# Head steps of a sliding-window attention kernel: a bank for the value product, and score maxima head by head in three banks

## The chip, the cores and the metric

The kernel runs on one core of a Trainium2 chip. The metric is the device time of one execution in microseconds (us). Before the change three runs took 2301.49, 2301.74 and 2302.6 us; the median is 2301.74.

A core has engines that run side by side, each with its own queue of instructions in program order: PE (TensorE) multiplies matrices, and PEld is its loading of weights; DVE (VectorE), ACT (ScalarE) and POOL (GpSimd) work on elements; SP issues the DMA transfers. PE writes into PSUM, which has eight banks of 512 fp32 columns on 128 partitions. Engines wait for each other on semaphores.

## The reference

Four layers act on x of 2048 rows and 640 columns; layers 1 and 3 are attention, layers 2 and 4 Fourier mixing:

```python
qkv = (x @ wqkv).reshape(B, S, 3, H, Dh).transpose(2, 0, 3, 1, 4)   # H = 32, Dh = 20
scores = einsum("bhqd,bhkd->bhqk", q, k) * Dh ** -0.5
mask = (idx[:, None] - idx[None, :] >= 0) & (idx[:, None] - idx[None, :] < 256)
p = softmax(where(mask, scores, -1e9))
o = einsum("bhqk,bhkd->bhqd", p, v).transpose(0, 2, 1, 3).reshape(B, S, D) @ wo
...
x = x + A(layernorm(x)); x = x + F(layernorm(x)); x = x + A(layernorm(x)); x = x + F(layernorm(x))
```

The change touches only the two attention layers. Each query row sees at most 256 keys, which is three blocks of 128 keys.

## The kernel before

**Quads, blocks and steps.** The 32 heads are taken in eight groups of four, called quads here (NQ = 8), and the 2048 rows in 16 blocks of 128 (NB = 16). A step of `heads` handles one block of one quad, so a layer has 128 steps. Of the four heads, two (z = 0 and 1) times two (e = 0 and 1), the index e says on which half of PE's rows a head's q and k lie (rows 0 or 64 onward): matmuls of different e can run side by side.

**Three strands in a step.** Each step serves three places at once. Strand s runs ten steps ahead (LEAD): `s_head` (the matmul at L545) computes the scores of one query block against up to three key blocks, and `s_max` takes the row maximum under the mask. For three key blocks `s_max` works on two heads, that is two banks, at once: L558 overwrites the masked part of the third block with a copy of the first, and L561 takes the maximum over columns 128 to 384. For the first two blocks of a quad (one or two key blocks) it runs one instruction per head, L564, which adds the mask, takes the maximum and leaves it in `mc`, and writes the masked scores to a scratch tile `ux` that nobody reads. Every four steps `m_rows` transposes the maxima of four blocks on PE (L571), copies them negated to `mt` on ACT (L574), and two DMAs (L576) put them as an extra row beside q. Strand t: `t_head` (L585) computes the scores transposed, with keys on the partitions and the maximum subtracted by that extra row; `t_exp` (L594, ACT) takes the exponential into `pt`; `t_mask` (L600, L604, POOL) sets masked entries to zero. Strand v is one step behind t: `pv` (L615) multiplies by the values of four heads side by side, each on 32 columns of PE, and L622 on ACT copies the result into `ou`.

**Banks.** Transposed scores go to banks 0 and 1, scores for maxima to banks 2 and 3 (z = 0) and 4 and 5 (z = 1). Bank 2 also takes the value product in its columns 384 to 512, and the transposition of `m_rows` in its first 128. Projections and other fill work use banks 6 and 7, and others while they are free; the table ROLES lists them.

**The order in a step** is written out by hand at the end of `heads`: for each z the four score matmuls in the order t (e=0), s (e=1), t (e=1), s (e=0), then `s_max`, `t_exp` and `t_mask`; after z = 0 comes `fill`, which issues a portion of other matmuls (the projections of later quads, L189, and later the partial sums of the output projection, whose results are added at L861); after z = 1 come the transposition (every fourth step), `pv` and the copy of the transposition. Work put off with `post` is issued some half steps later by `tick`. In the first head stage a fill has eight matmuls of 512 columns, in every fourth step six; in the late stage, when the projections are done, it has some 18 of 320 columns. `copied` (L474 on DVE, L476 on ACT, then L477 and L478 on POOL) empties a projection's banks every eight steps; L636 on DVE takes the reciprocals of the softmax sums every four steps.

Of the kernel before, what the change touches and what calls it, by code (L numbers as in the profile page):

```python
# [10 lines left out]
U16 = mybir.dt.uint16  # L11
AF = mybir.ActivationFunctionType
OP = mybir.AluOpType
AX = mybir.AxisListType
# [3 lines left out]
P = 128  # L18
# [9 lines left out]
NEG = -1.0e30  # L28
# [14 lines left out]
CHUNKS = ((0, 16, 0, 8), (0, 16, 8, 16), (16, 24, 0, 16), (24, 32, 0, 16), (0, 32, 16, 20))  # L43

ROLES = {
    "m": (6, 7), "f": (6, 7, 0, 1), "w": (3, 4, 5, 7),
    "q": (0, 1), "v": (5, 6, 7), "x4": (2, 3), "x1": (4,),
    "o": (5, 6),
    "y": (5, 6, 7, 0), "x1h": (4, 1),
# [12 lines left out]
class Net:  # L62
# [66 lines left out]
    def next(self, name):  # L129
        i = self.turn.get(name, 0)  # L130
        self.turn[name] = i + 1
        tiles = getattr(self, name)[:3]
        return tiles[i % len(tiles)]
# [387 lines left out]
    def heads(self, xsrc, xdst, hook):  # L521
        nc = self.nc
        qp = [t.rearrange("p (z s) -> p z s", z=2) for t in self.qp]
# [13 lines left out]
                                  self.vd[n // 4][:, n % 4 * 4:n % 4 * 4 + 4, :])  # L537

        mc = {}

        def s_head(quad, qb, z, e):
            n = min(qb + 1, 3)
            k0 = qb - n + 1
            b = 64 * e
            nc.tensor.matmul(  # L545
                self.banks[:, 2 + 2 * z + e, :n * P], qp[quad % 2][b:b + 60, z, qb * P:(qb + 1) * P],
                kp[quad % 2][b:b + 60, z, k0 * P:(qb + 1) * P], start=True, stop=True)

        def s_max(quad, qb, z):


            n = min(qb + 1, 3)
            if qb % 4 == 0 and z == 0:
                mc[quad, qb // 4] = pool.tile([P, 2, 2, 4], F32, name="mc", tag="mc")
            out = mc[quad, qb // 4][:, z, :, qb % 4]
            p = self.banks[:, 2 + 2 * z:4 + 2 * z, :]
            if n == 3:
                nc.vector.copy_predicated(  # L558
                    p[:, :, 256:384], self.mask[:, 256:].bitcast(U16).unsqueeze(1).broadcast_to([P, 2, P]),
                    p[:, :, :128])  # L560
                nc.vector.tensor_reduce(out=out, in_=p[:, :, 128:384], op=OP.max, axis=AX.X)  # L561
                return
            for e in range(2):
                nc.vector.tensor_tensor_reduce(  # L564
                    out=self.ux[:, :n * P], in0=p[:, e, :n * P], in1=self.mask[:, 384 - n * P:], scale=1.0, scalar=NEG,
                    op0=OP.add, op1=OP.max, accum_out=out[:, e:e + 1])

        def m_rows(quad, u):
            m = mc.pop((quad, u))
            p = self.banks[:16, 2, :P]  # L570
            nc.tensor.transpose(p, m.rearrange("p z e j -> p (z e j)"), self.ident)  # L571
            mt = pool.tile([16, P], F32R, name="mt", tag="mt", bufs=1)
            yield
            nc.scalar.activation(mt, p, AF.Copy, scale=-1.0)  # L574
            for z in range(2):
                self.post(1, lambda z=z: nc.sync.dma_start(  # L576
                    qp[quad % 2][60:125:64, z, u * 512:(u + 1) * 512].bitcast(F32),
                    mt[8 * z:8 * z + 8, :].bitcast(F32)))
# [3 lines left out]
        def t_head(quad, kb, z, e):  # L582
            n = min(NB - kb, 3)
            b = 64 * e
            nc.tensor.matmul(  # L585
                self.banks[:, e, :n * P], kp[quad % 2][b:b + 61, z, kb * P:(kb + 1) * P],
                qp[quad % 2][b:b + 61, z, kb * P:(kb + n) * P], start=True, stop=True)
# [19 lines left out]

        def pv(quad, qb):

            p = self.banks[:, 2, 384:]  # L610
            for kb in range(max(qb - 2, 0), qb + 1):
                t = pt[quad, kb]
                vq = self.vq[(4 * quad + kb // 4) % 3]
                for h in range(4):
                    nc.tensor.matmul(  # L615
                        p[32 * h:32 * h + 32, :], vq[:, 96 * (kb % 4) + 21 * h:96 * (kb % 4) + 21 * h + 32],
                        t[:, h, (qb - kb) * P:(qb - kb + 1) * P], start=kb == max(qb - 2, 0), stop=kb == qb,
                        tile_position=(0, 32 * h), skip_group_check=True)
            pt.pop((quad, qb - 2), None)
            if qb % 4 == 0:  # L620
                now_ou[0] = self.next("ou")
            nc.scalar.activation(now_ou[0][:, qb % 4 * P:qb % 4 * P + P], p, AF.Copy)  # L622
            if qb % 4 == 3:
                finish(quad, qb // 4, now_ou[0])

        now_ou = [None]

        def finish(quad, bk, ou):
            sm = pool.tile([P, 16], F32, name="sm", tag="sm")
            rc = pool.tile([P, 16], F32, name="rc", tag="rc")  # L630
            cols = slice(bk * 512, (bk + 1) * 512)
            at = (2, 7, 9) if quad < NQ - 1 else (1, 5, 6)
            self.post(at[0], lambda: nc.sync.dma_start(sm, ou[0:P:32, :]))
            self.post(at[0], lambda: nc.sync.dma_start(
                self.od[4 * quad:4 * quad + 4, :, cols].rearrange("h r s -> (h r) s"), ou))
            self.post(at[1], lambda: nc.vector.reciprocal(out=rc, in_=sm))  # L636

            def store():
                nc.sync.dma_start(
                    self.rd[bk, 4 * quad:4 * quad + 4, :].rearrange("h (a b) -> (h a) b", b=16), rc)  # L640
                self.stored.add((quad, bk))
            self.post(at[2], store)
# [33 lines left out]
        def fill(n):  # L676

            k, size = 0, 1
            while k < size:
                r = more()  # L680
                if r == 0 and k == 0:
                    continue
                if r != 1:
                    return
                k += 1
                if k == 1:
                    left = self.left + 1
                    size = -(-left // max(1, round(left / n)))
            if self.left == 0:
                more()  # L690
                relieve()
# [3 lines left out]
        steps = 16 * NQ  # L695
        for step in range(-LEAD, steps + 1):
            now[0] = step
            self.wide, self.lead, self.tiled = step + LEAD > steps, step < -2, step < steps - 1
            for f in later.pop(step, []):
                f()  # L700
            s, t, v = step + LEAD, step, step - 1
            if due and s >= due[0][0]:
                while done[0] < due[0][1]:
                    fill(15)
                due.pop(0)
                q, j = (s + AHEAD) // 16, (s + AHEAD) % 16 // 4
                for i, f in enumerate(self.pack(q, j)):
                    defer(i // 3, f)
                for f in later.pop(step, []):
                    f()  # L710
            if v >= 0 and v % 4 == 3:
                load_v(v // 4 + 2)
            if done[0] < total:
                nf = max([FIRST if t < 0 else RATE]
                         + [(d - done[0]) / max(1, at - s) for at, d in due])
            elif made[0] < early:
                nf = LATE
            else:
                nf = LATE
            rows = ((s - 1) // 16, ((s - 1) % 16) // 4) if 4 <= s < steps + 4 and s % 4 == 0 else None  # L720
            for z in range(2):
                for e in range(2):
                    if 0 <= t < steps:
                        t_head(t // 16, t % 16, z, e)
                    if 0 <= s < steps:
                        s_head(s // 16, s % 16, z, 1 - e)
                if 0 <= s < steps:
                    s_max(s // 16, s % 16, z)
                if 0 <= t < steps:
                    for e in range(2):  # L730
                        t_exp(t // 16, t % 16, z, e, e + 1)
                    t_mask(t // 16, t % 16, z)
                if z:
                    m = m_rows(*rows) if rows else iter(())
                    next(m, None)
                    if 0 <= v < steps:
                        pv(v // 16, v % 16)
                    for _ in m:
                        pass
                if z == 0 and t >= 0 or t < -1 or t >= steps:  # L740
                    fill(nf)
                self.tick()
            if step >= steps:
                self.load_to(step - steps + 2)
            if step > 16 * (NQ - 1):
                self.poll_late(step - 16 * (NQ - 1))
# [794 lines left out]
```

## Time and profile before

| What | us |
|---|---|
| median of three runs | 2301.74 |
| span of the profiled execution, from the first to the last instruction | 2300.9 |
| first head stage of the first attention layer | 172 to 440 |
| late head stage of the first attention layer | 456 to 534 |
| the same stages of the second attention layer | 1318 to 1580 and 1600 to 1675 |

The profile is one execution. A row of a group reads: line, engine, operation, written tile <- read tiles, shapes, count | busy us, mean ns of one | idle time of the engine just before, and what ended most of it. A row of the waits reads: who waited <- for whom: us in total, times, longest. A row of the timeline reads: start us, duration us, engine, line, operation, and in brackets the idle time before it. Starts of matmuls are recorded, their ends are modelled. The tile `banks` is the whole of PSUM, so rows don't name the bank.

### The profile page before, as it was taken

The numbers are of one execution on the slowest core, as the hardware profiler recorded it, in microseconds if no ns is written. First come the engines' busy times: TensorE is split into PE (matmuls) and PEld (weight loads), VectorE is DVE, ScalarE is ACT, GpSimd is POOL, SyncE is SP. The second block draws the span as 40 slices with busy tenths as digits, with TensorE's granted clock in tenths as the row PEclk, the third lists the DMA queues.
The fourth block names the chain that finished last, engine by engine and source line by source line (L and its number), as shares of the span: only waits on it lengthen the run. The fifth ranks groups of instructions, "written<-read, shape, count | busy, mean of one in ns | idle before, by whom it ended". The sixth has DMA issues, their size and how long they took to land.

```text
span 2300.9 us, 48611 instructions
## 1 busy us (share of the span) xinstructions
PE 2209.8 (96%) x18064; PEld 1844.4 (80%) x18064; DVE 1499.6 (65%) x2841; ACT 1114.3 (48%) x2497; POOL 1019.9 (44%) x1540
## 2 busy tenths in 40 slices
PE   8999999999889999999999999999988899999999
PEld 7977777677758888889999777776777688888899
DVE  6357777675688768772451677776747978688622
ACT  2117666666454545541331266666665545445310
POOL 3036666767745223230130466667677442331300
PEclk9999999999999999999999999999999999999999
DMA  5545556774535354655455455657744344546452
GB/s 189 173 148 168 182 166 192 218 195 146 175 112 176 126 179 137 212 166 177 149 168 181 144 183 166 190 185 218 199 153 151 111 164 142 178 141 214 157 171 98
DMA packets 217293, 385.53 MB, mean 168 GB/s; under 512 B 38880, under 2 KB 85472, under 8 KB 217056
## 3 DMA queue, kind: packets, MB, share of 16 engines
q1 hardware_dynamic: 217056, 382.43, 51.8%
q8 instruction: 142, 2.33, 0.4%
q14 instruction: 95, 0.78, 0.1%
HBM read 267.39 MB, written 113.77 MB: 166 GB/s over the span
## 4 chain that ended last, share of the span: by engine, by line
PE 39%; POOL 4%; DVE 3%; DMA 2%; ACT 2%; issue 1%; SPq 0%; POOLq 0%; ACTq 0%
PE banks L1234 14%; PE banks L171 11%; PE banks L189 5%; PE banks L615 3%; PE banks L585 3%; PE banks L545 2%; POOL big L164 1%; DMA qk_d<-c 1%; POOL c L478 0%; POOL x L783 0%; POOL pt L604 0%; DVE mc L561 0%; POOL kp L164 0%; POOL ou L1163 0%; POOL pt L600 0%
## 5 line engine op out<-in xcount | busy, mean ns | idle before, releaser
L594 ACT ACTIVATE pt<-banks 128x384 f32<-128x384 f32 (+2 forms) x1024 | 425.9, 468 | 191.4 <-PE banks L585 151.6
L545 PE MATMUL banks<-kp,qp 60*128 60x384 f32 (+2 forms) x1024 | 370.3, 381 | 3.8 <-DVE mc L561 1.9
L561 DVE TENSOR_REDUCE mc<-banks 128x2 f32<-128x512 f32 x448 | 310.4, 693 | 15.4
L600 POOL TENSOR_SCALAR_AFFINE_SELECT pt<-pt 128x256 f32<-128x256 f32 x512 | 208.8, 408 | 246.2 <-ACT pt L594 195.9
L189 PE MATMUL banks<-big,wc 64*128 64x512 f32 x1920 | 306.1, 402 | 0.4 <-DVE pt L372 0.4
L558 DVE COPY_PREDICATED banks<-mask,banks 128x256 f32<-128x256 uint16 x448 | 191.6, 428 | 152.8 <-PE banks L545 138.8
L585 PE MATMUL banks<-qp,kp 61*128 61x384 f32 (+2 forms) x1024 | 257.6, 363 | 7.9 <-ACT pt L594 7.0
L615 PE MATMUL banks<-pt,vq 128*32 128x128 f32 x5760 | 216.9, 279 | 17.2 <-DVE mc L561 11.9
L545 PEld LDWEIGHTS banks<-kp,qp 60*128 60x128 f32 x1024 | 182.6, 186 | 47.6 <-ACT ou L622 22.5
L189 PEld LDWEIGHTS banks<-big,wc 64*128 64x128 f32 x1920 | 210.5, 187 | 10.8 <-DVE pt L372 0.5
L615 PEld LDWEIGHTS banks<-pt,vq 128*32 128x32 f32 x5760 | 145.0, 110 | 78.6 <-DVE mc L561 46.1
L585 PEld LDWEIGHTS banks<-qp,kp 61*128 61x128 f32 x1024 | 148.9, 187 | 71.2 <-ACT pt L594 40.2
L164 DVE TENSOR_TENSOR qp<-pt,qp 128x512 fp32r<-128x512 f32 (+1 forms) x209 | 168.9, 816 | 47.8 <-ACT qp L158 46.9
L604 POOL TENSOR_SCALAR_AFFINE_SELECT pt<-pt 128x256 f32<-128x256 f32 x448 | 182.9, 408 | 0.0
L158 ACT ACTIVATE qp<-pt 128x512 fp32r<-128x512 f32 (+1 forms) x209 | 128.9, 624 | 99.5 <-DVE pt L1164 33.0
L1234 PE MATMUL banks<-qp,big 128*128 128x512 f32 x630 | 152.9, 393 | 6.1 <-POOL big L164 4.2
L1163 POOL TENSOR_TENSOR pt<-pt,pt 128x512 f32<-128x512 f32 x40 | 60.5, 1516 | 206.5 <-DMA pt<-c 148.0
L1422 DVE TENSOR_TENSOR x<-banks,x 128x320 f32<-128x320 f32 x64 | 29.7, 488 | 178.5 <-DMA x<-x_d 117.1
L1234 PEld LDWEIGHTS banks<-qp,big 128*128 128x128 f32 x630 | 118.2, 189 | 31.8 <-POOL big L164 5.7
L158 ACT ACTIVATE c<-pt 128x512 fp32r<-128x512 f32 x144 | 88.3, 624 | 75.0 <-DVE pt L1160 36.6
L164 DVE TENSOR_TENSOR c<-pt,c 128x512 fp32r<-128x512 f32 x140 | 110.1, 798 | 14.9 <-ACT c L158 12.6
L171 PE MATMUL banks<-big,pt 128*128 128x320 f32 x768 | 118.2, 309 | 0.7 <-DVE pt L1359 0.7
(204 smaller groups left out, 4527.7 us busy)
## 6 DMA issues: line engine op xcount, KB each, us to landing
pt<-c SPq DMA_DIRECT2D x188, 512.0 KB
qk_d<-c SPq DMA_DIRECT2D x80, 512.0 KB
kp<-qk_d SPq DMA_DIRECT2D x384, 80.0 KB
qp<-qk_d SPq DMA_DIRECT2D x384, 80.0 KB
kp<-u_d SPq DMA_DIRECT2D x32, 640.0 KB
o_d<-ou SPq DMA_DIRECT2D x64, 256.0 KB
x_d<-x SPq DMA_DIRECT2D x48, 320.0 KB
v_d<-pt SPq DMA_DIRECT2D x16, 768.0 KB
```

Source lines behind the costliest of these rows:

```text
L158: nc.scalar.activation(hi, src, AF.Copy, scale=-1.0 if neg else 1.0)
L164: (eng or nc.vector).tensor_tensor(out=lo, in0=src, in1=hi.bitcast(F32), op=OP.subtract)
L171: self.nc.tensor.matmul(p, x, y, start=n == 0, stop=n == last)
L189: self.nc.tensor.matmul(ps[a], x[r], y[r], start=half + i == 0, stop=half == 1 and i == n - 1, skip_group_check=True)
L545: nc.tensor.matmul(self.banks[:, 2 + 2 * z + e, :n * P], qp[quad % 2][b:b + 60, z, qb * P:(qb + 1) * P], kp[quad % 2][b:b + 60, z, k0 * P: ...
L558: nc.vector.copy_predicated(p[:, :, 256:384], self.mask[:, 256:].bitcast(U16).unsqueeze(1).broadcast_to([P, 2, P]), p[:, :, :128])
L561: nc.vector.tensor_reduce(out=out, in_=p[:, :, 128:384], op=OP.max, axis=AX.X)
L585: nc.tensor.matmul(self.banks[:, e, :n * P], kp[quad % 2][b:b + 61, z, kb * P:(kb + 1) * P], qp[quad % 2][b:b + 61, z, kb * P:(kb + n) * P ...
L594: nc.scalar.activation(pt[quad, kb][:, 2 * z + e0:2 * z + e1, :n * P], self.banks[:, e0:e1, :n * P], AF.Exp, scale=SCALE)
L600: nc.gpsimd.affine_select(out=t[:, :, 0:P], in_=t[:, :, 0:P], pattern=[[0, 2], [1, P]], compare_op=OP.is_ge, fill=0.0, base=0, channel_mul ...
L615: nc.tensor.matmul(p[32 * h:32 * h + 32, :], vq[:, 96 * (kb % 4) + 21 * h:96 * (kb % 4) + 21 * h + 32], t[:, h, (qb - kb) * P:(qb - kb + 1 ...
L1234: nc.tensor.matmul(self.banks[:, bk, :], p, b[q], start=start and m == 0, stop=stop and last and m == 2, skip_group_check=True)
```

## The change

The value product gets bank 5, each block of four at its own 128 columns, and ACT copies two blocks at a time, after every second one. The scores for maxima go to banks 2, 3 and 4 in turn, one bank a head (`s_bank`), and mask and maximum are one instruction per head for every block; it follows its score matmul directly in `s_head`, and `s_max` is gone. The transposition of the maxima takes a turn among the same three banks, and is issued, whole, after the value product. In the second half of each z the order of the two matmuls is exchanged: t (e=0), s (e=1), s (e=0), t (e=1). In the role "w", used once the score strand has ended, bank 2 replaces bank 5.

```diff
--- before.py
+++ after.py
@@ -43,7 +43,7 @@
 CHUNKS = ((0, 16, 0, 8), (0, 16, 8, 16), (16, 24, 0, 16), (24, 32, 0, 16), (0, 32, 16, 20))
 
 ROLES = {
-    "m": (6, 7), "f": (6, 7, 0, 1), "w": (3, 4, 5, 7),
+    "m": (6, 7), "f": (6, 7, 0, 1), "w": (2, 3, 4, 7),
     "q": (0, 1), "v": (5, 6, 7), "x4": (2, 3), "x1": (4,),
     "o": (5, 6),
     "y": (5, 6, 7, 0), "x1h": (4, 1),
@@ -537,40 +537,32 @@
                                   self.vd[n // 4][:, n % 4 * 4:n % 4 * 4 + 4, :])
 
         mc = {}
+        turn = [0]
+
+        def s_bank():
+            turn[0] += 1
+            return 2 + turn[0] % 3
 
         def s_head(quad, qb, z, e):
+
             n = min(qb + 1, 3)
             k0 = qb - n + 1
             b = 64 * e
+            p = self.banks[:, s_bank(), :n * P]
             nc.tensor.matmul(
-                self.banks[:, 2 + 2 * z + e, :n * P], qp[quad % 2][b:b + 60, z, qb * P:(qb + 1) * P],
+                p, qp[quad % 2][b:b + 60, z, qb * P:(qb + 1) * P],
                 kp[quad % 2][b:b + 60, z, k0 * P:(qb + 1) * P], start=True, stop=True)
-
-        def s_max(quad, qb, z):
-
-
-            n = min(qb + 1, 3)
-            if qb % 4 == 0 and z == 0:
+            if (quad, qb // 4) not in mc:
                 mc[quad, qb // 4] = pool.tile([P, 2, 2, 4], F32, name="mc", tag="mc")
-            out = mc[quad, qb // 4][:, z, :, qb % 4]
-            p = self.banks[:, 2 + 2 * z:4 + 2 * z, :]
-            if n == 3:
-                nc.vector.copy_predicated(
-                    p[:, :, 256:384], self.mask[:, 256:].bitcast(U16).unsqueeze(1).broadcast_to([P, 2, P]),
-                    p[:, :, :128])
-                nc.vector.tensor_reduce(out=out, in_=p[:, :, 128:384], op=OP.max, axis=AX.X)
-                return
-            for e in range(2):
-                nc.vector.tensor_tensor_reduce(
-                    out=self.ux[:, :n * P], in0=p[:, e, :n * P], in1=self.mask[:, 384 - n * P:], scale=1.0, scalar=NEG,
-                    op0=OP.add, op1=OP.max, accum_out=out[:, e:e + 1])
+            nc.vector.tensor_tensor_reduce(
+                out=self.ux[:, :n * P], in0=p, in1=self.mask[:, 384 - n * P:], scale=1.0, scalar=NEG,
+                op0=OP.add, op1=OP.max, accum_out=mc[quad, qb // 4][:, z, e, qb % 4:qb % 4 + 1])
 
         def m_rows(quad, u):
             m = mc.pop((quad, u))
-            p = self.banks[:16, 2, :P]
+            p = self.banks[:16, s_bank(), :P]
             nc.tensor.transpose(p, m.rearrange("p z e j -> p (z e j)"), self.ident)
             mt = pool.tile([16, P], F32R, name="mt", tag="mt", bufs=1)
-            yield
             nc.scalar.activation(mt, p, AF.Copy, scale=-1.0)
             for z in range(2):
                 self.post(1, lambda z=z: nc.sync.dma_start(
@@ -607,7 +599,7 @@
 
         def pv(quad, qb):
 
-            p = self.banks[:, 2, 384:]
+            p = self.banks[:, 5, qb % 4 * P:qb % 4 * P + P]
             for kb in range(max(qb - 2, 0), qb + 1):
                 t = pt[quad, kb]
                 vq = self.vq[(4 * quad + kb // 4) % 3]
@@ -619,7 +611,9 @@
             pt.pop((quad, qb - 2), None)
             if qb % 4 == 0:
                 now_ou[0] = self.next("ou")
-            nc.scalar.activation(now_ou[0][:, qb % 4 * P:qb % 4 * P + P], p, AF.Copy)
+            if qb % 2:
+                cs = slice(qb % 4 * P - P, qb % 4 * P + P)
+                nc.scalar.activation(now_ou[0][:, cs], self.banks[:, 5, cs], AF.Copy)
             if qb % 4 == 3:
                 finish(quad, qb // 4, now_ou[0])
 
@@ -720,23 +714,19 @@
             rows = ((s - 1) // 16, ((s - 1) % 16) // 4) if 4 <= s < steps + 4 and s % 4 == 0 else None
             for z in range(2):
                 for e in range(2):
-                    if 0 <= t < steps:
-                        t_head(t // 16, t % 16, z, e)
-                    if 0 <= s < steps:
-                        s_head(s // 16, s % 16, z, 1 - e)
-                if 0 <= s < steps:
-                    s_max(s // 16, s % 16, z)
+                    heads = [(t_head, t, e), (s_head, s, 1 - e)]
+                    for head, n, i in heads[::-1] if e else heads:
+                        if 0 <= n < steps:
+                            head(n // 16, n % 16, z, i)
                 if 0 <= t < steps:
                     for e in range(2):
                         t_exp(t // 16, t % 16, z, e, e + 1)
                     t_mask(t // 16, t % 16, z)
                 if z:
-                    m = m_rows(*rows) if rows else iter(())
-                    next(m, None)
                     if 0 <= v < steps:
                         pv(v // 16, v % 16)
-                    for _ in m:
-                        pass
+                    if rows:
+                        m_rows(*rows)
                 if z == 0 and t >= 0 or t < -1 or t >= steps:
                     fill(nf)
                 self.tick()
```

## The prediction

> **What bounds the kernel now.** I read the page first, then the table of waits, then the two head stages instruction by instruction, because an average over the span hides which wait closes a step.
>
> ```profile
> span 2300.9 us, 48611 instructions
> PE 2209.8 (96%) x18064; PEld 1844.4 (80%) x18064; DVE 1499.6 (65%) x2841; ACT 1114.3 (48%) x2497; POOL 1019.9 (44%) x1540
> L561 DVE TENSOR_REDUCE mc<-banks 128x2 f32<-128x512 f32 x448 | 310.4, 693 | 15.4
> ...
> L558 DVE COPY_PREDICATED banks<-mask,banks 128x256 f32<-128x256 uint16 x448 | 191.6, 428 | 152.8 <-PE banks L545 138.8
> ```
>
> PE looks full, but its ends are modelled, and a matmul that waits behind another can count as busy. So the waits at the head lines matter more than the 96%:
>
> ```profile
> PEld banks L615 <- DVE mc L561: 46.1, 120, 1.4
> PEld banks L545 <- ACT ou L622: 22.5, 134, 0.2
> PEld banks L545 <- ACT mt L574: 17.2, 55, 0.3
> PEld banks L571 <- DVE mc L561: 10.4, 36, 0.3
> ```
>
> Four waits return in nearly every step, and all four go over bank 2: the value product (L615) and the transposition (L571) wait for the maximum that reads banks 2 and 3, and the next score (L545) waits for the copies that empty bank 2. One ordinary step of the first head stage:
>
> ```profile
> 251.84 0.44 PE L585 MATMUL banks<-qp,kp 61*128 61x384 f32 x1
> 252.13 0.34 PE L585 MATMUL banks<-qp,kp 61*128 61x384 f32 x1
> 252.31 0.44 PE L545 MATMUL banks<-kp,qp 60*128 60x384 f32 x1
> 252.32 1.36 PE L189 MATMUL banks<-big,wc 64*128 64x512 f32 x8
> 252.79 0.43 DVE L558 COPY_PREDICATED banks<-mask,banks 128x256 f32<-128x256 uint16 x1 [0.51 <-PE banks L545]
> 253.25 0.69 DVE L561 TENSOR_REDUCE mc<-banks 128x2 f32<-128x512 f32 x1
> 253.35 0.33 PE L545 MATMUL banks<-kp,qp 60*128 60x384 f32 x1
> 253.52 0.34 PE L585 MATMUL banks<-qp,kp 61*128 61x384 f32 x2
> 253.70 0.33 PE L545 MATMUL banks<-kp,qp 60*128 60x384 f32 x1
> 254.00 0.86 PE L615 MATMUL banks<-pt,vq 128*32 128x128 f32 x24
> 254.79 0.38 PE L585 MATMUL banks<-qp,kp 61*128 61x256 f32 x1
> 254.93 0.28 ACT L622 ACTIVATE ou<-banks 128x128 f32<-128x128 f32 x1
> 255.26 0.44 PE L545 MATMUL banks<-kp,qp 60*128 60x384 f32 x1
> ```
>
> This is a closed loop: score 252.31, mask and maximum 252.79 to 253.94 (253.25+0.69), value product 254.00, its copy 254.93 to 255.21, next score 255.26. In sum 0.48+1.15+0.06+0.93+0.28+0.05 = 2.95 us, exactly the step. Neither PE nor DVE is full in it (DVE idles 0.51); the latency of the loop sets the step.
>
> **The change, part by part.**
>
> *Own bank for the value product; the transposition takes a turn among the score banks.* The loop is cut. What would PE need without it? The last score of the first half could follow the matmul at 252.13 on the other rows instead of coming at 252.31 (0.18). The value product could follow the score of 253.70 after one more interval as between 253.52 and 253.70 (0.18), so at some 253.9 instead of 254.00 (0.09). The step falls to 2.95-0.27 = 2.68. The eight projection matmuls take 253.35-252.32 = 1.03, 0.26 a pair; in four steps one step has six instead of eight (-0.26) and one a transposition (an estimate of 0.2, a little over a score's 0.18, since a weight load and a change of rows go with it). Four steps are some 4x2.68-0.26+0.2 = 10.7 us, sixteen some 42.6. Sixteen steps take today:
>
> ```profile
> 218.46 0.41 PE L615 MATMUL banks<-pt,vq 128*32 128x128 f32 x6
> ...
> 266.18 0.38 PE L615 MATMUL banks<-pt,vq 128*32 128x128 f32 x5
> ```
>
> that is 47.72 us (the product of a group's first block, then of the next group's). On PE alone, sixteen steps would win 5.1 us.
>
> *One mask-and-maximum instruction per head.* It has never run on 384 elements here, but the first two blocks of each group use it on 128 and 256:
>
> ```profile
> 231.95 0.29 DVE L564 CUSTOM_DVE_ANT_0 ux<-banks,mask 128x128 bf16<-128x128 f32 x1 [0.60 <-PE banks L545]
> 232.29 0.29 DVE L564 CUSTOM_DVE_ANT_0 ux<-banks,mask 128x128 bf16<-128x128 f32 x1
> ...
> 235.07 0.42 DVE L564 CUSTOM_DVE_ANT_0 ux<-banks,mask 128x256 bf16<-128x256 f32 x1 [1.25 <-PE banks L545]
> 235.43 0.08 DVE L564 DVE_READ_ACCUMULATOR2_ANT mc<- 128x1 f32 x1
> 235.54 0.42 DVE L564 CUSTOM_DVE_ANT_0 ux<-banks,mask 128x256 bf16<-128x256 f32 x1
> 235.89 0.08 DVE L564 DVE_READ_ACCUMULATOR2_ANT mc<- 128x1 f32 x1
> 236.12 0.42 DVE L564 CUSTOM_DVE_ANT_0 ux<-banks,mask 128x256 bf16<-128x256 f32 x1
> 236.47 0.08 DVE L564 DVE_READ_ACCUMULATOR2_ANT mc<- 128x1 f32 x1
> 236.59 0.42 DVE L564 CUSTOM_DVE_ANT_0 ux<-banks,mask 128x256 bf16<-128x256 f32 x1
> ...
> 235.75 0.28 PE L545 MATMUL banks<-kp,qp 60*128 60x256 f32 x1
> ```
>
> Each head is two DVE instructions, the sweep and the read of its accumulator. From start to start a pair takes 0.34 on 128 and 0.47 on 256 elements; the same 0.13 more gives 0.60 on 384. That is the lower bound. But the interval 235.54 to 236.12 is 0.58, 0.11 longer. The third sweep is the first of its pair: it waits for PE as well as for the sweep before it, whose scratch ux it overwrites. The score at 235.75 ended at 236.03, 0.09 before it, while the predicated copy above follows its score (252.31+0.44 = 252.75) by 0.04; so PE alone doesn't explain the 0.11, and I read most of it as the price of waiting for two engines. After the change every head has both waits. Upper bound: 0.60+0.11 = 0.71 per head. I take 0.71, since the new instruction is of the kind of the one that shows it.
>
> Sixteen steps hold 56 heads of 384, four of 256 and four of 128: 56x0.71+4x0.58+4x0.45 = 43.9 us of DVE. Between them come two projection copies, priced by the predicated copy that follows one:
>
> ```profile
> 247.96 0.68 DVE L474 COPY x<-banks 128x512 f32<-128x512 f32 x1
> 248.56 0.42 DVE L558 COPY_PREDICATED banks<-mask,banks 128x256 f32<-128x256 uint16 x1
> ```
>
> 2x0.60 = 1.2, and four reciprocals, which I estimate at 0.15 each beside the accumulator read, 0.6. DVE needs 45.7 us of sixteen steps, against 42.6 on PE: DVE becomes the bound. For bubbles I add 0.3 (the transposition holds one of three banks for part of a step). 46.0 against 47.72: 1.7 us won per sixteen steps. The lower bound 0.60 gives 56x0.60+4x0.47+4x0.34+1.8 = 38.6, below PE's 42.6.
>
> The Trainium skill, VectorE: DVE Perf Modes, section "The DRAIN you can't avoid", reports that chained Vector instructions with a semaphore after each took as long as with one at the end. By that rule 0.60 would hold; the interval 235.54 to 236.12 here speaks against it, and the rule's result is the first rival.
>
> *Three banks in turn instead of four in pairs.* A head waits for the maximum three heads earlier. With DVE the bound, PE runs ahead until the banks are full; three waiting heads are 2.1 us of DVE work. PE's longest absence is the fill: 0.17 for the score before it, 1.03, and 0.48 from a score to DVE, 1.7. Three banks cover that by 0.4, so I price the rotation at nothing in this stage. In the late stage, where the fill is longer, the cover is thin:
>
> ```profile
> 172.00:440.00 268.00, 262.76 (x3422) 199.47 (x3419) 199.43 (x439) 187.02 (x496) 183.31 (x398) 1.00 0.58 181
> ...
> 456.00:534.00 78.00, 75.03 (x1058) 58.98 (x1057) 58.84 (x126) 48.31 (x128) 52.78 (x99) 1.00 0.70 191
> ...
> L861 DVE TENSOR_TENSOR big<-banks,big 128x320 f32<-128x320 f32 x22 | 9.8, 486 | 0.9 <-PE banks L189 0.6
> ...
> L164 DVE TENSOR_TENSOR qp<-cr,qp 128x320 fp32r<-128x320 f32 x2 | 1.9, 974 | 1.7 <-ACT qp L158 1.7
> ```
>
> (columns of the first two: length, then PE, PEld, DVE, ACT, POOL; the last two are of the late window). There some 22 steps need 22/16x43.9 = 60.4 for heads, 9.8 for the partial sums at L861, 1.9 for weight splits and some 1.5 for reciprocals: 74 of 78 us. I forecast no change there, with bounds of 6 us won (22x0.27, the loop alone cut) and 10 lost (rival two).
>
> *Order of the heads, and who else waits.* The second score now precedes the second transposed score; both row halves keep the same work, so nothing is gained or lost. Two copies of 128 columns (0.28 each) become one of 256: no more than 0.56 per two steps, hidden, since the bank has four slots and the next write to the same columns is four steps away; ACT is busy 187 of 268 us. The transposition moves behind the value product. Its copy was already behind the product's copy on ACT, and its two DMAs are still posted one half step later; behind them on SP wait the packing loads:
>
> ```profile
> SPq L576 <- ACT pt L594: 51.2, 23, 4.1
> ```
>
> SP already waits 2.2 us for these rows each time, so some tenths more fall on loads issued blocks ahead. I price this at nothing; if that cover were gone, it would be at most 0.3 x 32 x 2 = 19 us. Roles of the banks after the heads only exchange 5 for 2: nothing. In the steps before the maxima meet the value product PE is full of projection work, and nothing is won.
>
> **Sum.** The first head stage of a layer is 268/47.72 = 5.6 groups; 5.6x1.7 = 9.5 us per layer, 19 for both attention layers. The profiled execution's 2300.9 becomes 2282; the median of the runs, 2301.74, lies 0.8 above the span. Predicted: **2283 us**.
>
> **Rivals.**
>
> *PE becomes the bound.* If a head costs 0.60, PE's 42.6 decides: 5.1x5.6 = 29 us per layer, plus up to 4 of the late stage: 2302-66 = 2236. For it: the plain 0.60 between sweeps that wait once, and a page's rule. Against: the 0.58 interval.
>
> *Nothing measurable.* DVE at 0.74 per head: 47.4+0.3 for sixteen steps equals today's 47.7; 2302. For it: the 0.71 is already within 4% of that.
>
> *Slower: DVE runs dry behind three banks.* Place: the fill of the late stage and the steps with a transposition, where two banks serve. The late fill has 18 matmuls of 320 columns instead of 8 of 512, so 1.03x18/8x320/512 = 1.5; PE is away for 0.17+1.5+0.48 = 2.15 us, against 2.1 of queued heads, and with a bank held by the transposition 1.4. A bubble of some 0.5 in each of 22 steps is 10 us per layer. It outweighs the gain when the first stage wins under that, from 0.71 per head upwards with L861's sums queued among the heads; at 0.73 (sixteen steps 47.1) it is +10-0.6x5.6 = +7 per layer, 2315. Against it: the first stage's fill is short, and its cover of 0.4 holds.
>
> **How the numbers follow.** DVE the bound at about 0.71: 0.48, with a range of its own of 2270 to 2296. PE the bound, 2225 to 2260: 0.20. Nothing measurable: 0.14. Slower: 0.18. A measurement of this kernel tells 0.2% (4.6 us) from no change. Faster is 0.48+0.20 = 0.68; same 0.14; slower 0.18. The range runs from the PE-bound case, 2234, to near the slower case, 2312; what is left out below and above is about 0.2.
>
> **What would show it.** Right: the waits of L615 on the maximum and of L545 on the copies of bank 2 are gone; sweeps on 384 elements start 0.71 apart, with the accumulator read between; the step is near 2.87, and PE's waits at L545 name the accumulator read three heads earlier. Wrong: sweeps 0.60 apart, or PE steps of 2.68; DVE idle before sweeps in most steps (rival three); or value products that now wait for POOL's masks, since the step shortened. The forecast falls with the 0.11.

## The result and the profile after

The changed kernel took 2282.3 us (median of four runs, 2281.5 to 2289.7) against 2302.2 of the kernel before beside it (2301.5 to 2303.7). The ratio is 0.9920, with a 95% interval of 0.9906 to 0.9935. Run again with other experiments it took 2284.3, a ratio of 0.9928 (0.9913 to 0.9942).

In the changed kernel the score matmul of `s_head` is L552, the sweep (mask and maximum) L557, the transposition L564, the transposed score L577, the exponential L586, the masks L592 and L596, the value product L607, its copy L616 and the reciprocal L630. The page's busy shares, and its group of sweeps:

```profile
span 2280.3 us, 50212 instructions
PE 2185.6 (96%) x18064; PEld 1811.8 (79%) x18064; DVE 1512.0 (66%) x3737; ACT 1106.0 (49%) x2369; POOL 1004.1 (44%) x1540
L557 DVE CUSTOM_DVE_ANT_0 ux<-banks,mask 128x384 bf16<-128x384 f32 (+2 forms) x1024 | 545.1, 532 | 186.5 <-PE banks L552 53.0 <-PE banks L577 16.9 <-PE banks L607 0.5
```

PE shows 96% before and after, though the kernel is 20 us shorter: the share tells nothing of the bound. DVE's busy time rose by 12 us while the time fell, so less work on DVE isn't what was won. The table of waits:

```profile
PEld banks L552 <- DVE mc L557: 61.6, 175, 1.0
...
PEld banks L607 <- POOL pt L592: 13.9, 26, 1.2
...
PEld banks L564 <- DVE mc L557: 4.7, 20, 0.4
```

The value product no longer waits for a maximum, nor the score for the copies `ou` and `mt`: three of the four waits quoted before are gone, and the transposition's fell from 10.4 us to 4.7. What is left at the score is a wait for the maximum three heads earlier, that is, for a bank. DVE (VectorE) in the first head stage:

```profile
240.69 0.56 DVE L557 CUSTOM_DVE_ANT_0 ux<-banks,mask 128x384 bf16<-128x384 f32 x1
241.18 0.08 DVE L557 DVE_READ_ACCUMULATOR2_ANT mc<- 128x1 f32 x1
241.40 0.56 DVE L557 CUSTOM_DVE_ANT_0 ux<-banks,mask 128x384 bf16<-128x384 f32 x1
...
242.11 0.56 DVE L557 CUSTOM_DVE_ANT_0 ux<-banks,mask 128x384 bf16<-128x384 f32 x1
...
242.82 0.56 DVE L557 CUSTOM_DVE_ANT_0 ux<-banks,mask 128x384 bf16<-128x384 f32 x1
```

From start to start it is 0.71 three times (240.69, 241.40, 242.11, 242.82). Four heads are 2.84 us, the ordinary step. PE over the same time, and the value products sixteen steps apart:

```profile
214.31 0.42 PE L607 MATMUL banks<-pt,vq 128*32 128x128 f32 x8
...
226.05 0.85 PE L607 MATMUL banks<-pt,vq 128*32 128x128 f32 x20
227.28 0.41 PE L607 MATMUL banks<-pt,vq 128*32 128x128 f32 x4 [0.38 <-POOL pt L592]
...
242.02 0.44 PE L552 MATMUL banks<-kp,qp 60*128 60x384 f32 x1 [0.27 <-DVE mc L557]
...
260.55 0.42 PE L607 MATMUL banks<-pt,vq 128*32 128x128 f32 x8
```

Sixteen steps take 46.24 us here (214.31 to 260.55), 47.72 before. At 242.02 PE waits for a bank that DVE has not left. At 227.28 the last four matmuls of a value product wait 0.38 for a mask on POOL; this returns once in sixteen steps.

PE isn't always the one that waits. In the sixteen steps from 214.31 to 260.55 DVE waits for PE 2.4 us in all:

```profile
DVE ux L557 <- PE banks L552: 1.5, 5, 0.5
DVE ux L557 <- PE banks L577: 0.9, 1, 0.9
```

All but one of these waits lie between 227.7 and 233.6, around the first two blocks of a quad, where a head has 128 or 256 elements and costs DVE 0.44 or 0.57: there PE is behind, and POOL's 0.38 at 227.28 holds it further.

Where the time went, by stage. The limits are starts of value products in the trace, in each attention layer those of the first, the 92nd and the 128th step: 91 steps of the first head stage and 36 of the late stage. Times in us; the two numbers of a cell are the two attention layers. The rows e1 to e9 are the experiments below.

| kernel | up to the heads | 91 steps | 36 late steps | between the layers' heads | after the heads |
|---|---|---|---|---|---|
| before | 169.2 | 273.7, 275.1 | 123.6, 122.8 | 742.4 | 594.1 |
| after | 167.9 | 265.0, 264.4 | 120.9, 121.2 | 744.6 | 596.2 |
| after, run again | 171.2 | 265.1, 264.6 | 122.8, 120.8 | 745.1 | 596.2 |
| e1, in place | 172.6 | 250.4, 252.3 | 124.8, 125.1 | 743.9 | 594.1 |
| e2, old banks, single | 169.0 | 267.4, 268.7 | 122.3, 122.0 | 741.8 | 595.6 |
| e3, old order | 168.1 | 263.8, 263.3 | 121.1, 121.6 | 744.5 | 593.5 |
| e4, more DVE | 168.1 | 300.9, 301.8 | 125.1, 126.9 | 742.0 | 593.9 |
| e5, late reciprocal | 170.8 | 250.3, 250.5 | 120.5, 118.8 | 742.8 | 593.1 |
| e6, old banks, in place | 167.3 | 269.2, 268.2 | 126.2, 122.2 | 744.0 | 596.0 |
| e7, later splits | 184.2 | 246.3, 246.0 | 122.3, 119.8 | 757.4 | 594.2 |
| e8, later splits, not in the lead | 172.6 | 247.8, 246.5 | 120.2, 118.9 | 742.6 | 592.2 |
| e9, two banks | 171.7 | 277.8, 279.2 | 127.0, 126.4 | 746.4 | 596.8 |

From before to after the 91 steps won 8.7 and 10.7, the late steps 2.7 and 1.6. The last two columns lost 2.2 and 2.1; no instruction there was changed. The loss returned when the changed kernel was run again (745.1 and 596.2), but e4, whose code there is the same, doesn't show it (742.0 and 593.9).

### The profile page after: what moved, and what is told of

Read it like the earlier page. It is cut to its first block, busy times and chain, and to the rows that moved or that the text cites. A ratio compares the mean times of both kernels' runs of the same rounds, so it can differ in the third digit from the quotient of the medians.

```text
span 2280.3 us, 50212 instructions
## 1 busy us (share of the span) xinstructions
PE 2185.6 (96%) x18064; PEld 1811.8 (79%) x18064; DVE 1512.0 (66%) x3737; ACT 1106.0 (49%) x2369; POOL 1004.1 (44%) x1540
## 4 chain that ended last, share of the span: by engine, by line
PE 36%; POOL 5%; DVE 4%; DMA 2%; issue 2%; ACT 1%; SPq 0%; DVEq 0%; POOLq 0%; ACTq 0%
PE banks L1224 14%; PE banks L171 11%; PE banks L189 4%; PE banks L607 3%; DVE ux L557 2%; PE banks L577 2%; PE banks L552 2%; POOL big L164 1%; POOL c L478 1%; POOL pt L592 0%; POOL pt L596 0%; DMA rr<-r_d 0%; POOL kp L164 0%; POOL x L773 0%; DMA kp<-qk_d 0%
## 5 line engine op out<-in xcount | busy, mean ns | idle before, releaser
L557 DVE CUSTOM_DVE_ANT_0 ux<-banks,mask 128x384 bf16<-128x384 f32 (+2 forms) x1024 | 545.1, 532 | 186.5 <-PE banks L552 53.0
L586 ACT ACTIVATE pt<-banks 128x384 f32<-128x384 f32 (+2 forms) x1024 | 435.8, 469 | 223.2 <-PE banks L552 118.5
L577 PE MATMUL banks<-qp,kp 61*128 61x384 f32 (+2 forms) x1024 | 329.7, 383 | 8.9 <-ACT pt L586 8.5
L552 PE MATMUL banks<-kp,qp 60*128 60x384 f32 (+2 forms) x1024 | 313.3, 377 | 19.5 <-DVE mc L557 18.8
L592 POOL TENSOR_SCALAR_AFFINE_SELECT pt<-pt 128x256 f32<-128x256 f32 x512 | 210.2, 411 | 224.3 <-ACT pt L586 185.9
L189 PE MATMUL banks<-big,wc 64*128 64x512 f32 x1920 | 263.0, 391 | 0.4 <-DVE pt L372 0.4
L577 PEld LDWEIGHTS banks<-qp,kp 61*128 61x128 f32 x1024 | 179.4, 185 | 68.9 <-ACT pt L586 40.0
L552 PEld LDWEIGHTS banks<-kp,qp 60*128 60x128 f32 x1024 | 172.8, 185 | 74.8 <-DVE mc L557 61.6
L607 PE MATMUL banks<-pt,vq 128*32 128x128 f32 x5760 | 217.2, 278 | 7.8 <-POOL pt L592 7.8
L164 DVE TENSOR_TENSOR qp<-pt,qp 128x512 fp32r<-128x512 f32 (+1 forms) x209 | 173.2, 837 | 50.0 <-ACT qp L158 49.0
L189 PEld LDWEIGHTS banks<-big,wc 64*128 64x128 f32 x1920 | 184.3, 186 | 20.4 <-DVE pt L372 0.5
L607 PEld LDWEIGHTS banks<-pt,vq 128*32 128x32 f32 x5760 | 144.2, 110 | 61.9 <-issue 46.7
L596 POOL TENSOR_SCALAR_AFFINE_SELECT pt<-pt 128x256 f32<-128x256 f32 x448 | 184.2, 411 | 0.0
L1224 PE MATMUL banks<-qp,xc 128*128 128x512 f32 x480 | 119.0, 395 | 0.0
L164 DVE TENSOR_TENSOR c<-pt,c 128x512 fp32r<-128x512 f32 x140 | 107.9, 783 | 15.1 <-ACT c L158 12.7
```

What stands on the lines that cost most here:

```text
L164: (eng or nc.vector).tensor_tensor(out=lo, in0=src, in1=hi.bitcast(F32), op=OP.subtract)
L189: self.nc.tensor.matmul(ps[a], x[r], y[r], start=half + i == 0, stop=half == 1 and i == n - 1, skip_group_check=True)
L552: nc.tensor.matmul(p, qp[quad % 2][b:b + 60, z, qb * P:(qb + 1) * P], kp[quad % 2][b:b + 60, z, k0 * P:(qb + 1) * P], start=True, stop=True)
L557: nc.vector.tensor_tensor_reduce(out=self.ux[:, :n * P], in0=p, in1=self.mask[:, 384 - n * P:], scale=1.0, scalar=NEG, op0=OP.add, op1=OP. ...
L577: nc.tensor.matmul(self.banks[:, e, :n * P], kp[quad % 2][b:b + 61, z, kb * P:(kb + 1) * P], qp[quad % 2][b:b + 61, z, kb * P:(kb + n) * P ...
L586: nc.scalar.activation(pt[quad, kb][:, 2 * z + e0:2 * z + e1, :n * P], self.banks[:, e0:e1, :n * P], AF.Exp, scale=SCALE)
```

## The experiments

Each ratio is against the kernel before, run beside it on the same chip. e1, e3, e4 and e9 are edits of the changed kernel, e2 and e6 of the kernel before; e5 builds on e1, and e7 and e8 on e5.

**e1: what do the sweeps wait for?** The masked scores are written back into their own bank, not into the shared scratch `ux`. Then no sweep overwrites what the one before it wrote, and the wait on DVE itself goes; the wait on PE stays.

```diff
-                out=self.ux[:, :n * P], in0=p, in1=self.mask[:, 384 - n * P:], scale=1.0, scalar=NEG,
+                out=p, in0=p, in1=self.mask[:, 384 - n * P:], scale=1.0, scalar=NEG,
```

> Edit: the sweep for the maximum writes its masked scores back into the score bank instead of the shared scratch tile ux, so that it no longer has to wait for the sweep before it; it keeps its wait for PE. Theory A (DVE is the bound, and 0.11 us of each 0.71 us is the second wait): sweeps on 384 elements follow each other at some 0.60 us, PE becomes the bound, sixteen steps of the first stage fall from 46.2-47.0 us to 42.6-44, and the time to 2240-2255. Rival B (the rotation of three banks sets the step, not DVE's occupancy): the sweeps wait longer for PE instead, and the time stays at 2277-2287. Rival C (the 0.11 belongs to the instruction, not to the wait): sweeps stay 0.71 apart, 2282.

2261.9 us, ratio 0.9821 (0.9793 to 0.9849). That is above the 2240 to 2255 of theory A. A stretch of DVE in its late stage, with one row of SP:

```profile
448.36 0.57 DVE L557 CUSTOM_DVE_ANT_0 banks<-banks,mask 128x384 f32<-128x384 f32 x1 [1.00 <-PE banks L577]
448.85 0.14 DVE L557 DVE_READ_ACCUMULATOR2_ANT mc<- 128x1 f32 x1
448.85 0.60 DVE L557 CUSTOM_DVE_ANT_0 banks<-banks,mask 128x384 f32<-128x384 f32 x1
449.36 0.14 DVE L557 DVE_READ_ACCUMULATOR2_ANT mc<- 128x1 f32 x1
...
450.10 0.62 SPq L627 DMA_DIRECT2D sm<-ou  x1
...
454.84 0.25 DVE L630 RECIPROCAL rc<-sm 128x16 f32<-128x16 f32 x1 [5.33 <-DMA sm<-ou]
```

The next sweep starts with the accumulator read (448.85), 0.49 after the one before. So the wait on DVE itself was 0.71-0.49 = 0.22 of each head, twice the 0.11 that theory A gave it. A step of the 91 is 250.4/91 = 2.75 us on the mean, against 2.91 in the changed kernel (265.0/91), and the 91 steps win another 14.6 and 12.1: DVE was the bound there. The late stage gives 4 us per layer back, and the last two rows say why: the reciprocal is issued a fixed number of half steps behind the DMA that brings its data, and the faster DVE came to it at 449.50, before SP had even issued that DMA (450.10). For 5.33 us it stood in front of all sweeps.

**e2: the single instructions alone, in the old banks.**

```diff
-            if n == 3:
-                nc.vector.copy_predicated(
...
-                nc.vector.tensor_reduce(out=out, in_=p[:, :, 128:384], op=OP.max, axis=AX.X)
-                return
             for e in range(2):
```

> Edit: the kernel before, with all its banks, its order and its copies, but the maximum for three key blocks taken by one sweep per head as for the first two blocks. Theory A: the old loop gets shorter, because the value product now waits for one sweep of bank 2 instead of a pair of instructions over banks 2 and 3 (0.48+0.57+0.06+0.93+0.28+0.05 = 2.37 us), and DVE at four times 0.71 = 2.84 us is the bound here too: 2278-2292, nearly all of the whole change's gain without a bank moved. Rival D (the gain comes from the bank of its own and the copies, and the single instruction by itself costs): 2302 or more.

2288.6 us, ratio 0.9943 (0.9921 to 0.9966), within theory A's range; the step is 2.91. One of them (here the score is L545, the sweep L558, the value product L609):

```profile
258.48 0.44 PE L545 MATMUL banks<-kp,qp 60*128 60x384 f32 x1
...
258.96 0.56 DVE L558 CUSTOM_DVE_ANT_0 ux<-banks,mask 128x384 bf16<-128x384 f32 x1
...
259.56 0.56 DVE L558 CUSTOM_DVE_ANT_0 ux<-banks,mask 128x384 bf16<-128x384 f32 x1
...
259.87 0.33 PE L545 MATMUL banks<-kp,qp 60*128 60x384 f32 x1
260.05 0.08 DVE L558 DVE_READ_ACCUMULATOR2_ANT mc<- 128x1 f32 x1
...
260.13 0.86 PE L609 MATMUL banks<-pt,vq 128*32 128x128 f32 x24
...
261.06 0.28 ACT L616 ACTIVATE ou<-banks 128x128 f32<-128x128 f32 x1
...
261.39 0.44 PE L545 MATMUL banks<-kp,qp 60*128 60x384 f32 x1
...
261.87 0.56 DVE L558 CUSTOM_DVE_ANT_0 ux<-banks,mask 128x384 bf16<-128x384 f32 x1 [0.43 <-PE banks L545]
```

The loop over bank 2 is still there, from score to score 2.91, and DVE idles 0.43 in it, so it isn't the bound that theory A made it. From the score at 258.48 to the value product at 260.13 two ways take the same time: over DVE, to the end of the second sweep's read (260.05+0.08 = 260.13), and over PE, whose last score came at 259.87. The wait on its own shows here as well: the second sweep of a pair starts 0.60 after the first (258.96 to 259.56).

**e6: the same with the sweeps in place.** It tells whether DVE sets the step of e2.

```diff
-                    out=self.ux[:, :n * P], in0=p[:, e, :n * P], in1=self.mask[:, 384 - n * P:], scale=1.0, scalar=NEG,
+                    out=p[:, e, :n * P], in0=p[:, e, :n * P], in1=self.mask[:, 384 - n * P:], scale=1.0, scalar=NEG,
```

> Edit: e2 (old banks, one sweep per head) with the sweep in place, so that DVE needs far less. Theory A: in the old layout a second loop stands right behind the first, and DVE is not in it: first score, fill, second half's scores, value product, its copy out of bank 2, next first score, 2.91 us in e2's profile. Then a faster DVE changes nothing here: 2283-2290; the bank of its own is what cuts this loop, and it is worth 2288-2262 = 26 us as soon as DVE is not the bound. Rival: e2 was bound by DVE like the changed kernel, and in place it comes to 2260-2270 without a bank moved.

2290.9 us, ratio 0.9948 (0.9931 to 0.9964): no faster than e2. Its sweeps are 0.48 apart (259.25 and 259.73 below), but the loop stands:

```profile
258.77 0.44 PE L545 MATMUL banks<-kp,qp 60*128 60x384 f32 x1
...
259.25 0.57 DVE L558 CUSTOM_DVE_ANT_0 banks<-banks,mask 128x384 f32<-128x384 f32 x1 [0.34 <-PE banks L545]
...
259.73 0.60 DVE L558 CUSTOM_DVE_ANT_0 banks<-banks,mask 128x384 f32<-128x384 f32 x1
...
260.41 0.86 PE L609 MATMUL banks<-pt,vq 128*32 128x128 f32 x24
...
261.34 0.28 ACT L616 ACTIVATE ou<-banks 128x128 f32<-128x128 f32 x1
...
261.67 0.18 PEld L545 LDWEIGHTS banks<-kp,qp 60*128 60x128 f32 x1 [0.16 <-ACT ou L616]
```

The step is 2.90 (258.77 to 261.67), and at its end the score waits for the value product's copy. The four kernels together, in us:

| | scratch shared by all sweeps | sweeps in place |
|---|---|---|
| value product in bank 2 (e2, e6) | 2288.6 | 2290.9 |
| a bank of its own and the rest of the change (after, e1) | 2282.3 | 2261.9 |

Neither half wins alone what both win together: with bank 2 the loop is the bound and a faster DVE is worth nothing; with the own bank DVE is the bound, and the own bank looks like 6 us instead of 29. The 6 is not clear of noise (run again, the changed kernel took 2284.3, and its interval overlaps with that of e2); the 29 is.

**e4: two columns of `ux` set to zero after each sweep**, a little more DVE work per head.

```diff
                 op0=OP.add, op1=OP.max, accum_out=mc[quad, qb // 4][:, z, e, qb % 4:qb % 4 + 1])
+            nc.vector.memset(self.ux[:, :2], 0.0)
```

> Edit: the changed kernel with one more small DVE instruction per head, a memset of two elements of ux behind each sweep. Theory A: each head's interval on DVE grows by what it costs, and the step by four times that, with no slack: with 0.1 us a head some 470 heads of two layers give 94 us, 0.2 us gives 190; the time is 2282 plus 940 times the measured growth of the interval. Rival B: part of the growth disappears in DVE's idle time, and the time grows by clearly less than 940 times it.

2362.4 us, ratio 1.0263 (1.0232 to 1.0294). Two neighbouring sweeps of it:

```profile
244.46 0.56 DVE L557 CUSTOM_DVE_ANT_0 ux<-banks,mask 128x384 bf16<-128x384 f32 x1
...
245.09 0.06 DVE L560 MEMSET ux<- 128x1 uint32 x1
245.30 0.56 DVE L557 CUSTOM_DVE_ANT_0 ux<-banks,mask 128x384 bf16<-128x384 f32 x1
```

A head takes 0.84, 0.13 more. On 4x91 heads that would be 47 a layer if DVE set every step; 35.9 and 37.4 came, more than three quarters. So DVE is the bound in most of the first head stage, not in all of it. The rest went into waits: DVE waits for PE 16.8 us in this stage of the first layer in the changed kernel, and 2.6 here. Theory A, with no slack at all, is wrong by that much. In the late stage 4x36x0.13 = 19 would have come, and 4.2 and 5.7 did: there DVE mostly isn't the bound.

**e9: two banks in turn instead of three.**

```diff
-            return 2 + turn[0] % 3
+            return 2 + turn[0] % 2
```

> The changed kernel with its scores for maxima in two banks in turn instead of three. Theory (the third bank is the cover over PE's absence in the fill: two waiting heads are 2 x 0.71 = 1.42 of DVE work against 0.17 + 1.03 + 0.48 = 1.7 of absence): DVE idles some 0.3 in each step of the first head stage, 91 x 0.3 = 27 a layer, and 0.7 in each of the 36 late steps, 26 a layer at most; 2337 with the first stage alone, up to 2390. Rival (the cover isn't needed, since ACT, POOL or PE set the step or matmuls of the other rows pass the waiting score): 2280 to 2290.

2329.3 us, ratio 1.0114 (1.0097 to 1.0131), slower than the kernel before. The sweep behind the fill:

```profile
242.03 0.56 DVE L557 CUSTOM_DVE_ANT_0 ux<-banks,mask 128x384 bf16<-128x384 f32 x1
...
242.91 0.56 DVE L557 CUSTOM_DVE_ANT_0 ux<-banks,mask 128x384 bf16<-128x384 f32 x1 [0.31 <-PE banks L552]
```

It comes 0.88 after the one before instead of 0.71: DVE runs dry by 0.17 a step, about half of the 0.3 expected, and the 91 steps lose 12.8 and 14.8, the late ones 6.1 and 5.2. The mechanism of the third rival exists, at two banks. That three cover it is shown by the 0.71 at the same place in the changed kernel.

**e3: the order of the heads as before.**

```diff
-                    for head, n, i in heads[::-1] if e else heads:
+                    for head, n, i in heads:
```

> Edit: the changed kernel with the old order of the four score matmuls in a half step (t e=0, s e=1, t e=1, s e=0). Theory A: DVE is the bound and has heads waiting; no change, 2279-2286. Rival: the new order lets the sweep start earlier and is worth 0.17 us a half step where DVE runs dry; then 2290 or more.

2278.8 us, ratio 0.9904 (0.9883 to 0.9925). The interval overlaps with both of the changed kernel's: the new order wins nothing, and by the times alone it is not settled whether it costs 0.1 to 0.2%. In the traces the old order is a little shorter in both 91-step stretches (263.8 and 263.3 against 265.0 and 264.4).

**e5: e1 with the reciprocal and its store four half steps later.**

```diff
-            at = (2, 7, 9) if quad < NQ - 1 else (1, 5, 6)
+            at = (2, 11, 13) if quad < NQ - 1 else (1, 5, 6)
```

> Edit: e1 (sweep in place) with the reciprocals of the softmax sums, and their store, issued four half steps later (11 and 13 instead of 7 and 9). In e1 the first head stage won 23 us per layer against before, but the late stage lost 1 to 2, and in it DVE stood 5.3 us behind a reciprocal that waited for the DMA of its sums. Theory A: with shorter steps a fixed number of half steps no longer covers that DMA, and every score behind the reciprocal waits; issued later it is hidden again: 2253-2258, and DVE's waits for that DMA, 11.7 us in four cases, fall below 2. Rival: the late stage is held by something else (exponentials, masks, partial sums), and the time stays at 2260-2264.

2248.4 us, ratio 0.9771 (0.9757 to 0.9786), below the 2253 to 2258 expected. The late stage wins 4.3 and 6.3 and is now better than before the change: e1's loss there was the early reciprocal. What PE still waits for at the value product is POOL:

```profile
PEld banks L607 <- POOL pt L592: 18.3, 16, 2.2
```

One such place on the timeline, POOL's rows and PE's:

```profile
225.48 1.02 POOL L164 TENSOR_TENSOR wc<-x,wc 128x384 fp32r<-128x384 f32 x1
226.44 0.42 POOL L592 TENSOR_SCALAR_AFFINE_SELECT pt<-pt 128x256 f32<-128x256 f32 x1
...
226.91 0.41 PE L607 MATMUL banks<-pt,vq 128*32 128x128 f32 x4 [0.73 <-POOL pt L592]
```

The mask that the value product needs stands behind a split of weights for the next projection (L164, 1.02 us) and ends at 226.86, 0.05 before PE goes on. In the first layer's 91 steps this is there once in sixteen.

**e7 and e8: the weight splits six half steps later**, in e7 everywhere, in e8 only among the heads.

```diff
-                self.post(3 * i, lambda ks=ks: self.split(w[:, 0, ks], w[:, 1, ks], raw[:, ks], eng=self.nc.gpsimd))
+                self.post((0 if self.lead else 6) + 3 * i, lambda ks=ks: self.split(w[:, 0, ks], w[:, 1, ks], raw[:, ks], eng=self.nc.gpsimd))
```

(This is e8; e7 has `6 + 3 * i`.)

> Edit: e5 with the splitting of the next projection weights issued six half steps later. In e1 the value product waits for POOL's masks once in sixteen steps, 1.1 us, where the weight splits follow two projection splits on POOL. Theory A: apart from each other they are covered, 1.1 us times 5.6 groups times two layers is 12 us less than e5. Rival: POOL has no room to catch up elsewhere, or the weights come late for the projections; no gain or a loss against e5.

> The weight splits are put off by six half steps only once the lead up to the heads is over; in the lead they stay where the run with the later reciprocals (2248.4) has them. Theory (the main stage holds PE up where value products wait for POOL's masks behind a weight split, and what the put-off splits lost lay in the lead alone): lead and middle return to 171 and 743, the main stages stay at 246; 2248.4 less 2 x 4.2 = 2240, 2236 to 2245. Rival (weights also come late for the projections among the heads, or the gain of the main stage came from what the lead had pushed back): 2248 or more.

e7: 2271.6 us, ratio 0.9869 (0.9854 to 0.9884), slower than e5, as its rival had it. Its 91 steps win 4.0 and 4.5 against e5, but the lead ahead of each layer's heads loses 13.4 and 14.6, since its projections now wait for their weights:

```profile
PEld banks L189 <- POOL wc L164: 25.0, 4, 7.1
```

e8: 2243.3 us, ratio 0.9738 (0.9724 to 0.9753), as expected (2240, 2236 to 2245). The lead's loss is gone, the 91 steps keep 2.5 and 4.0, and the value product's waits for POOL fell from sixteen to six:

```profile
PEld banks L607 <- POOL pt L592: 8.1, 6, 2.0
...
217.33 0.43 PE L607 MATMUL banks<-pt,vq 128*32 128x128 f32 x8
...
260.18 0.32 PE L607 MATMUL banks<-pt,vq 128*32 128x128 f32 x4
```

(the last two rows are of the timeline). Sixteen steps take 42.85. This is the fastest kernel of the study, 39 us below the changed one.

## Why the prediction was right, point by point

**The loop is cut.** Right. The waits that closed it are gone from the table, and e6 shows that with the loop in place a faster DVE is worth nothing.

**DVE becomes the bound at 0.71 per head.** Right, and the term on which the forecast stood. The sum gave 46.0 for sixteen steps; 46.24 was measured between the two value products quoted, 265.0/91x16 = 46.6 as a mean. 9.5 us per layer were forecast for the first head stage, 8.7 and 10.7 came. e1 and e4 show that DVE is the bound in most of it: the stage's time follows a change of DVE's time per head in both directions.

Part of this hit is luck, in two places. First, two terms of the sum were off in opposite directions, the 1.8 for copies and reciprocals and the 0.3 for bubbles:

```profile
243.31 0.69 DVE L474 COPY x<-banks 128x512 f32<-128x512 f32 x1
243.91 0.55 DVE L557 CUSTOM_DVE_ANT_0 ux<-banks,mask 128x384 bf16<-128x384 f32 x1
...
244.61 0.56 DVE L557 CUSTOM_DVE_ANT_0 ux<-banks,mask 128x384 bf16<-128x384 f32 x1
...
245.10 0.25 DVE L630 RECIPROCAL rc<-sm 128x16 f32<-128x16 f32 x1
245.32 0.56 DVE L557 CUSTOM_DVE_ANT_0 ux<-banks,mask 128x384 bf16<-128x384 f32 x1
```

The copy starts 0.49 after the sweep at 242.82, and the next sweep 0.60 later: together 0.38 more than 0.71, where the sum put 0.60. The reciprocal fits into the 0.71 of its sweep (244.61 to 245.32) and adds nothing. So copies and reciprocals add some 0.8 to sixteen steps, 1.0 less than the sum had. The bubbles are 1.2 more: DVE's six waits for PE are 2.4 us there, of which 0.14 each is the ordinary gap behind an accumulator read (241.26 to 241.40), and 1.5 is left. Second, the groups of sixteen steps did not win alike. The second to the fifth won 0.8 to 1.5 each, 1.3 on the mean, against the 1.7 forecast; the first won 2.9 and 4.6 (it took 49.26 and 50.58 before, 46.39 and 46.02 after) and made up for them. Why the first was so long before the change stays open.

**Where the 0.71 comes from.** I read 0.60 as a sweep that waits once and 0.11 as the price of waiting for two engines. The runs split it further: 0.48 with no wait (second of a pair in e6), 0.49 with the wait on PE alone (e1), 0.60 with the wait on DVE's own sweep alone (second of a pair in e2), 0.71 with both. The queue of DVE shows the second wait as an instruction of its own in front of nearly every one of the 1024 sweeps; the first row is of the changed kernel, the second of e1:

```profile
L557 DVEq EVENT_SEMAPHORE  x1022: 21/21/1487, 125.4 to 1653.3; - x171
L557 DVEq EVENT_SEMAPHORE  x58: 21/21/21, 178.1 to 1628.6; - x58
```

Writing in place also moved the output into PSUM and made it fp32; no run parts this from the wait, but the sweep itself got no shorter by it. My lower bound of 0.60 was no floor: it held one wait already. The Trainium skill, VectorE: DVE Perf Modes, section "The DRAIN you can't avoid", reports that eight chained copies took as long with a semaphore after each as with one after the last. Between these sweeps a wait on the engine's own result does cost: 0.12 by itself (0.48 to 0.60), 0.22 beside the wait on PE (0.49 to 0.71).

**PE alone: 42.6 for sixteen steps.** About right, though the changed kernel doesn't reach it: e8, in which DVE waits for PE 5.3 us of these sixteen steps and so is no bound, has 42.85. The rival that rested on it failed by its condition (0.60 per head), not by its size.

**The rotation at nothing.** Right in the ordinary steps of the first head stage, where sweeps stay 0.71 apart. It is not shown for the first two blocks of a quad, where DVE runs dry; whether a fourth bank would help there wasn't tried. The working was too dark: by it two banks would lose 0.3 a step, and e9 lost 0.17 in the step shown, so PE's absence is some 1.42+0.17 = 1.6 instead of 1.7, and the cover of three banks 0.5 instead of 0.4.

**The late stage at no change.** Off by a little: 2.7 and 1.6 us won, within the bounds of 6 won and 10 lost. I had DVE nearly full there (74 of 78 us); e4 shows that it isn't the bound, since only a quarter of the added work shows, and in the changed kernel it waits 34 of the 121 us of these steps.

**The value product and POOL.** Named among what would be wrong, and not priced. It is there once in sixteen steps (0.38 at 227.28) and becomes the next limit as soon as DVE is faster (e5 to e8).

**The order of the heads and the copies at nothing.** e3 agrees for the order, to within 0.2%. The copies and the transposition's move were not tried alone; the profile shows no wait of their own that is new. The stages between and after the heads lost 2.2 and 2.1, as much as the late stages won, so that the sum came out nearer than its terms; the change of ROLES alone isn't behind this loss, since e4, e5 and e8 have it too and don't show it (742.0 to 742.8 and 592.2 to 593.9).

## What to carry to other kernels

When a loop through a shared buffer sets the step, cut it and lower the next bound together: here the faster sweeps were worth nothing without the own bank, the own bank (with the rest of the change) some 6 us with the slow sweeps and 29 with the fast ones, so tested one at a time either may look useless. A sum over many steps hides those with another limit: DVE set most of the sixteen steps here, and PE the two with short rows. A result that nobody reads still orders the instructions that write it; a scratch tile shared by all is a chain, and writing in place took 20 us off for one argument. Once steps shorten, look at everything that is issued at a fixed distance in steps (a reciprocal behind its DMA, weight splits in front of masks): these distances were times once.

## What the runs showed of the hardware

- A sweep of 384 elements lasts 0.56 to 0.60 us, but the next can start 0.48 to 0.49 after it, together with the read of its accumulator (259.73 in e6, 448.85 in e1), if it has no wait on DVE's own results. The read itself then lasts 0.14 instead of 0.08.
- Writing fp32 into PSUM instead of bf16 into the scratch made the sweep hardly longer (0.57 to 0.60 against 0.56).
- An instruction that waits for a DMA holds up its engine whole: the reciprocal of e1 kept every sweep behind it for 5.33 us, though none of them needs it.
